# The transfer queue of a one-core attention and MLP kernel is put in the program's order

## The chip, the core and the metric

The kernel runs on one core of a Trainium2 chip. Its time is the device time of one launch in microseconds (us), the median of several runs. A core has five engines that each execute their own instructions in order: TensorE (PE in the profile; its weight loads are PEld), VectorE (DVE), ScalarE (ACT), GpSimd (POOL) and SyncE (SP). In this kernel SP computes nothing: it issues the transfers (DMAs), and SPq in the profile is its queue.

## What is computed

Attention with a top-32 mask over 8 batches, 8 heads, 576 rows and a head size of 64, and behind it a two-layer MLP with a smooth ReLU over 4608 tokens (512 to 2048 to 512), all in float32:

```python
scores = scale * np.matmul(q, k.transpose(0, 1, 3, 2))
kth = np.partition(scores, -top_k, axis=-1)[..., -top_k:-top_k + 1]
scores = np.where(scores >= kth, scores, -1000000000.0)
attn = np.exp(scores - np.max(scores, axis=-1, keepdims=True))
attn = attn / (np.sum(attn, axis=-1, keepdims=True) + 1e-09)
x = np.matmul(attn, v)                       # then (B, H, S, D) -> (B*S, H*D)
h = x @ w_in
g = np.where(h >= 1, h, np.where(h <= -1, 0.0, (h + 1) ** 2 / 4))
out = g @ w_out
```

## The kernel before

**Steps.** The work is cut into 144 steps. A step takes 128 query rows of one pair of heads. For each step PE computes the scores (`sp`, L354); ACT copies them to SBUF (`s`, L355) and takes the exponential (`e`, L391); DVE finds the 32 largest by repeated maxima and replacements (`more`, `less`, `tops`, L368 to L442) and masks the exponentials (L454); POOL divides by the sum (L407). Then the weights have to be transposed for the product with v (`po`, L502), whose result ACT copies into `xT` (L515). When a block of 128 tokens is complete, its MLP is queued: `ph` (L535), the activation by ACT (`r` L539, `g` L546) and POOL (L551 to L553), `py` (L558), and the output `y` (L561, L563).

**Early and late steps.** In the first steps PE transposes the weights, since it has time there while the MLP's own weights are being loaded and converted. In the late steps (about 144 to 1440 us) the transfers do it, in `move_w` (L480): ACT splits the weights into 16-bit halves (L484, two copies into the only buffer `halves`), a DMA writes them to DRAM (`rows`, L486), and a transposing DMA reads them back (`wT`, L488). Queries and keys of the batches from the third on go the same way in `turn` (L275): ACT's `parts` (L279), the write of `lines` (L281), and a transposing read into `qT` or `kT` (L282), which is kept in a list `turns` and issued by `finish_turns` (L286), either from `move_w` ahead of its own read or from slot 3 of a step.

**Inspection.** A late step of odd number also inspects a piece of the MLP's weights for values near zero: ACT reads the raw words twice (L172). The piece is loaded into a single buffer `raw` (L133); the call that loads it stands in slot 3 of the even step before (L770). There are 64 such pieces.

**Loads.** `load_values` (L189) is a generator: each `next` issues one group of the next batch's `v_in` or `v_tail`. `turned_keys_of` (L290) loads a `k_block` (three DMAs) and turns the one loaded before. `queries` (L680) turns a query block and calls `fetch` (L660), which loads the one after the next.

**The order.** The main loop (L737) goes through the steps, each in seven slots: slot 1 prepares queries and keys or values, slot 2 issues products with v and the scores of the step after the next, slot 3 has the inspection and `move_w` of the step before, and `advance` fills PE with MLP work in every slot. `tc.manual_schedule` (L654) makes PE, DVE, ACT and POOL execute their instructions in the order in which this loop writes them. SP is not on that list: a scheduler orders its transfers by their dependencies and its own estimates, and issues many loads well before the place at which the loop writes them.

Of the kernel before, what the change touches and what calls it, by code (L numbers as in the profile page):

```python
# [26 lines left out]
def kernel(  # L27
# [98 lines left out]
    def load(pool, i, bufs=3, parts=1):  # L126
        if i < n_pieces * parts and i not in loaded:
            if room:
                loaded[i] = room[i % len(room)]
            else:  # L130
                loaded[i] = pool.tile([P, 2 * WC // parts], U32, name="raw", bufs=min(bufs, 2))
            c = i % parts * (WC // parts)
            nc.sync.dma_start(out=loaded[i], in_=pieces_of_weights[i // parts][1][:, c:c + WC // parts].bitcast(U32))  # L133
# [42 lines left out]
    def run(ctx, paired):  # L176
# [104 lines left out]
            nc.sync.dma_start(out=lines, in_=parts)  # L281
            turns.append(partial(nc.sync.dma_start_transpose, dst.bitcast(U16), lines.rearrange("p t k -> (p t) k")))  # L282

        turns = []

        def finish_turns():  # L286
            while turns:
                turns.pop(0)()

        def turned_keys_of(b):  # L290

            kT = stage.tile([P, NHP, S], F32, name="kT")
            got = dict(kT=kT)

            def load_block(c):
                x = stage.tile([P, H, D], F32, name="k_block", tag="k_in")
                ends = k[b, :, SM:S, :].rearrange("h p d -> p h d")
                if c < NT:
                    nc.sync.dma_start(out=x[:, 0::2, :], in_=whole(k, b)[:, 0::2, c, :])
                    nc.sync.dma_start(out=x[TL:P, 1::2, :], in_=whole(k, b)[0:P - TL, 1::2, c, :])  # L300
                else:
                    nc.sync.dma_start(out=x[0:TL, 0::2, :], in_=ends[:, 0::2, :])
                nc.sync.dma_start(out=x[0:TL, 1::2, :], in_=whole(k, b)[P - TL:P, 1::2, c - 1, :] if c else ends[:, 1::2, :])
                return x

            blocks = {0: load_block(0)}
            got["loads"] = load_values(b)
            got["v"], got["v_tl"] = next(got["loads"])
            yield got
            for c in range(NT + 1):  # L310
                if c < NT:
                    blocks[c + 1] = load_block(c + 1)
                n = P if c < NT else TL
                turn(blocks.pop(c)[0:n], kT[:, :, c * P:c * P + n])
                yield got
# [164 lines left out]
        def move_w(st):  # L480
            st["wT"] = wT = late.tile([P, BLOCKS, P], F32, name="wT", bufs=4)
            halves = late.tile([P, 2, 2 * S], U16, name="halves")
            for i in range(2):
                nc.scalar.copy(halves[:, :, i * S:(i + 1) * S], st["e"][:, i, :].bitcast(U16).rearrange("p (k t) -> p t k", t=2))  # L484
            rows = dram.tile([P, 2, 2 * S], U16, name="rows")
            nc.sync.dma_start(out=rows, in_=halves)  # L486
            finish_turns()
            nc.sync.dma_start_transpose(wT.bitcast(U16), rows.rearrange("p t k -> (p t) k"))  # L488

        def block(i, c):  # L490
            return i * (NT + 1) + c if c < NT else NT
# [153 lines left out]
        def advance(amount, until):  # L645
# [4 lines left out]
            while pending and due >= pending[0][0] and pe_time < until and take():  # L650
# [1 line left out]
            due = min(due, 24.0)  # L652

        order = tc.manual_schedule(engines={mybir.EngineType.PE, mybir.EngineType.DVE, mybir.EngineType.Activation,  # L654
                                            mybir.EngineType.Pool})
        order.__enter__()
        keys, xTs = {}, {}
        q_ins, qTs = {}, {}
# [1 line left out]
        def fetch(i):  # L660
            if i < len(rounds) and rounds[i] not in q_ins:
                q_ins[rounds[i]] = load_queries(*rounds[i])
# [17 lines left out]
        def queries(m):  # L680
            nonlocal pe_time
            if m < n and steps[m][0:2] not in qTs:
                r = steps[m][0:2]
                if r[0] > 1:
                    qTs[r] = turned_queries_of(q_ins[r], r[1])
                else:
                    qTs[r] = queries_of(q_ins[r], r[1], nc.vector.tensor_copy if m == 0 else nc.scalar.copy)
                    pe_time += 0.5
                fetch(rounds.index(r) + 2)

        def begin(m):
            b, t, hp, ch, col = steps[m]
# [44 lines left out]
        for m in range(n + 2):  # L737
            early = converted < n_pieces
            if not early and first_late is None:
                first_late = m  # L740
            elif not early and late is None:
                conversion.close()
                room.clear()
                late = ctx.enter_context(tc.tile_pool(name="late", bufs=1))

            share, left = (total - spent) / (n + 2 - m), sum(x[0] for x in pending)
            for r in sorted(ready):
                if r + 4 > m and r >= valued:
                    share = min(share, left / (r + 4 - m))
                    left += NK * NF + NF * DM // P  # L750
            top_k, parts = None, [0] * SLOTS
            if m < n:
                top_k = weights(state[m], state[m - 1] if m > 0 else None, state[m + 1] if m + 1 < n else None)
                parts = [1] * SLOTS if early else [1, 1, 0, 1, 1, 1, 1]
                start = max(dve_time, scored[m])
                now_converting = range(0, SLOTS, 2)
                dve_time = start + K_TIME + PIECE_TIME * min(len(now_converting), n_pieces - converted)
                done[m] = dve_time
                state[m]["by_tensor"] = early or m >= n - 2
            for slot in range(SLOTS):  # L760
                now = start + (dve_time - start) * (slot + 1) / SLOTS
                for _ in range(parts[slot]):
                    next(top_k, None)
                if m < n and converted < n_pieces:
                    if slot in now_converting:
                        convert(now)
                elif slot == 3 and late is not None:
                    if m % 2:
                        inspect()
                    elif paired:  # L770
                        load(late, inspected, 1, 2)
                if slot == 1 and 1 <= m <= n and state[m - 1]["by_tensor"]:
                    pe_time = max(pe_time, done[m - 1] + 2.0) + 1.0
                    transpose_w(state[m - 1])
                    ready_at[m - 1] = pe_time + 1.8
                if slot == 3 and 1 <= m <= n and state[m - 1] is not None and not state[m - 1]["by_tensor"]:
                    move_w(state[m - 1])
                    ready_at[m - 1] = done[m - 1] + 15.0
                if slot == 3:
                    finish_turns()  # L780
                if slot == 2 and m == n and paired:
                    judge(ps, att)
                if slot == 2 and (early or m == first_late or m >= n - 1):
                    values_until(m)
                if m == 0 and slot in (1, 2):
                    next(first)
                if slot == 2 and not early:
                    if m % 2 == 0:
                        while pending and taken is not None and taken.__name__ == "hidden" and take():
                            pass  # L790
                    values_until((m - 2) // 2 * 2)
                if slot == (4 if early else 2):
                    begin_at(m + 2)
                if slot == (6 if early else 1):
                    queries(m + 3)
                    if (m < n and prep is None and next_keys < B and steps[m][0] == next_keys - 1 and steps[m][1] >= 1
                            and (next_keys > 1 or converted == n_pieces)):
                        prep = (turned_keys_of if next_keys > 1 else keys_of)(next_keys)
                    if prep is not None and (m % 2 == 0 or next_keys == 1):
                        got = next(prep, None)  # L800
                        pe_time += 0.5 if next_keys < 2 else 0.0
                        if got is None:
                            prep, next_keys = None, next_keys + 1
                        else:
                            keys[next_keys] = got
                            value_loads = got.get("loads", value_loads)
                    elif value_loads is not None:
                        next(value_loads, None)
                advance((EARLY_SHARE if early else share) / SLOTS if m < n else 32.0, now)
            for _ in (top_k if top_k is not None else ()):  # L810
                pass
# [50 lines left out]
```

## Time and profile before

| | us |
|---|---|
| median of 3 runs | 1506.48 (1506.18 to 1512.55) |
| the profiled execution, own time | 1507.81 |
| its span, first to last instruction | 1506.0 |
| PE, DVE, ACT, POOL busy | 1441.7, 1411.9, 1158.4, 908.5 |
| PEld busy (beside PE) | 1034.8 |
| SP's DMAs, share of 16 engines' span | 66.3% |

The profile is a page about one execution. Its first part gives the busy time of each engine, its fifth the groups of equal instructions (line, engine, operation, output and inputs, count; then busy time and mean ns of one; then the idle time just before them and what ended most of it), its sixth the DMA issues with the median time from issue to landing. Further views of the same trace are used below: busy time in stretches of the span; the waits of a stretch ("engine line waited for: us in total, times, longest"); and timelines of one engine, with the start and the duration of each instruction or row of equal ones. In SP's timeline a duration is that of the issue, not of the transfer: the data land later. A transposing read takes SP 2.3 to 3.4 us to issue, the write of `rows` 0.34 to 0.55.

The long middle of the run repeats every four steps in 38.3 us.

### The profile page before, as it was taken

What the parts mean: (1) busy time and instruction counts of PE and PEld (TensorE: products, weight loads), DVE (VectorE), ACT (ScalarE), POOL (GpSimd) and SP (SyncE); (2) the same over time, 40 slices, a digit from 0 to 9 for tenths busy, and PEclk for the clock granted to TensorE, in tenths of its full rate; (3) what the DMA queues carried; (4) which work ended last, traced back from release to release, by engine and by line L of the source; (5) the groups of instructions that cost most, each with busy time, mean ns of one, the idle gap of its engine ahead of it and who ended that gap; (6) DMA issues with size and microseconds to landing.
All of it is one profiled execution on the core that took longest, in us unless ns stands there. A gap on an engine that the chain in (4) does not pass through costs nothing.

```text
span 1506.0 us, 31908 instructions
## 1 busy us (share of the span) xinstructions
PE 1441.7 (96%) x10605; PEld 1034.8 (69%) x10605; DVE 1411.9 (94%) x4392; ACT 1158.4 (77%) x2221; POOL 908.5 (60%) x1309
## 2 busy tenths in 40 slices
PE   5698899999999999999999999999999999999998
PEld 3476577677777777677777777767777777777675
DVE  6989999999999999999999999999999999999912
ACT  6887788877778888687778888788778887877732
POOL 3463566666666666556666666666666666666630
PEclk6799899999999999999999999999999999999999
DMA  8632667785667787886677796787667877655510
GB/s 255 199 116 86 158 165 185 196 196 152 172 189 200 201 189 185 211 197 182 164 197 186 202 199 184 200 219 183 165 192 186 203 183 183 163 156 144 142 32 17
DMA packets 510318, 260.93 MB, mean 173 GB/s; under 512 B 460992, under 2 KB 469184, under 8 KB 510144
## 3 DMA queue, kind: packets, MB, share of 16 engines
q1 hardware_dynamic: 510144, 258.80, 66.3%
q8 instruction: 86, 1.41, 0.4%
q14 instruction: 88, 0.72, 0.1%
HBM read 62.91 MB, written 102.63 MB: 110 GB/s over the span
## 4 chain that ended last, share of the span: by engine, by line
PE 66%; DVE 20%; ACT 6%; DMA 3%; issue 3%; POOL 1%; SPq 1%; ACTq 0%; POOLq 0%
PE ph L535 24%; PE py L558 24%; PE sp L354 8%; PE po L502 8%; DVE more L375 5%; DVE e L454 4%; DVE less L368 2%; DVE more L368 2%; DMA rows<-halves 2%; PE pw L469 2%; DVE tops L416 2%; DVE tops L424 2%; DVE tops L435 2%; DVE seconds L442 2%; DVE tops L388 1%
## 5 line engine op out<-in xcount | busy, mean ns | idle before, releaser
L535 PEld LDWEIGHTS ph<-xT,w_in 128*128 128x128 f32 x4608 | 548.5, 193 | 100.0 <-issue 78.6
L535 PE MATMUL ph<-xT,w_in 128*128 128x128 f32 x4608 | 558.0, 277 | 1.3 <-ACT g L546 0.7
L558 PE MATMUL py<-w_out,g 128*128 128x512 f32 x1152 | 556.4, 603 | 1.7 <-ACT y L561 1.7
L551 POOL TENSOR_SCALAR r<-r 128x256 f32<-128x256 f32 x276 | 146.8, 532 | 453.6 <-ACT r L539 453.4
L375 DVE MATCH_REPLACE8 more<-tops,more 128x288 f32<-128x288 f32 x864 | 374.9, 437 | 0.0
L558 PEld LDWEIGHTS py<-w_out,g 128*128 128x128 f32 x1152 | 195.2, 190 | 166.9 <-issue 158.6
L484 ACT COPY halves<-e 128x1152 uint16<-128x1152 uint16 x268 | 293.6, 1143 | 13.4 <-DMA rows<-halves 13.4
L454 DVE SCALAR_TENSOR_TENSOR e<-s,kth,e 128x577 f32<-128x577 f32 x288 | 259.6, 937 | 0.8 <-ACT e L391 0.6
L553 POOL TENSOR_TENSOR g<-r,g 128x256 f32<-128x256 f32 x280 | 240.9, 860 | 22.0
L407 POOL TENSOR_SCALAR e<-e,rz 128x576 f32<-128x576 f32 x268 | 223.4, 843 | 12.6 <-DVE rz L400 12.6
L391 ACT ACTIVATE e<-s,nmax 128x576 f32<-128x576 f32 x288 | 222.5, 773 | 4.7
L539 ACT ACTIVATE r<-ph,half 128x256 f32<-128x256 f32 (+1 forms) x296 | 135.7, 458 | 116.4 <-PE ph L535 92.3
L355 ACT ACTIVATE s<-sp 128x576 f32<-128x576 f32 x288 | 171.9, 648 | 57.3 <-PE sp L354 55.6
L552 POOL TENSOR_TENSOR r<-r 128x256 f32<-128x256 f32 x276 | 190.1, 689 | 23.0
L354 PE MATMUL sp<-kT,qT 64*128 64x288 f32 x1024 | 164.1, 437 | 10.6 <-ACT kT L257 8.4
L502 PEld LDWEIGHTS po<-wT,v_in 128*64 128x64 f32 x2048 | 116.0, 139 | 60.5 <-ACT g L546 47.3
L502 PE MATMUL po<-wT,v_in 128*64 128x128 f32 x2048 | 142.1, 280 | 10.0 <-ACT g L546 6.5
L354 PEld LDWEIGHTS sp<-kT,qT 64*128 64x128 f32 x1024 | 89.7, 189 | 73.6 <-ACT r L539 28.0
L368 DVE TENSOR_TENSOR more<-s 128x576 f32<-128x576 f32 x144 | 112.3, 780 | 19.9 <-ACT s L355 19.9
L546 ACT ACTIVATE g<-ph,minus 128x256 f32<-128x256 f32 x280 | 129.8, 464 | 0.0
L416 DVE MAX8 tops<-more 128x8 f32<-128x288 f32 x288 | 125.4, 442 | 0.0
L368 DVE TENSOR_TENSOR less<-s 128x576 f32<-128x576 f32 x144 | 122.4, 850 | 0.0
(88 smaller groups left out, 1349.4 us busy)
## 6 DMA issues: line engine op xcount, KB each, us to landing
rows<-halves SPq DMA_DIRECT2D x134, 576.0 KB, 3.0
lines<-parts SPq DMA_DIRECT2D x48, 256.0 KB, 2.9
q_in<-in_q_dram SPq DMA_DIRECT2D x32, 256.0 KB, 3.7
v_in<-in_v_dram SPq DMA_DIRECT2D x32, 256.0 KB, 4.1
out_dram<-y SPq DMA_DIRECT2D x32, 256.0 KB, 2.8
raw<-in_moe_w_in_dram SPq DMA_DIRECT2D x32, 256.0 KB, 3.2
raw<-in_moe_w_out_dram SPq DMA_DIRECT2D x32, 256.0 KB, 3.3
kT<-in_moe_w_in_dram SPq DMA_DIRECT2D x8, 512.0 KB, 4.8
```

The source lines that it names most:

```text
L354: nc.tensor.matmul(*x, start=True, stop=True)
L368: nc.vector.tensor_tensor(out=x, in0=s[:, :, 0:SH], in1=s[:, :, SH:S], op=op)
L375: nc.vector.match_replace(out=st["rest"][:, i, :], in_to_replace=eight(st["tops"], i, r - 8), in_values=src[:, i, :], imm_value=LOWEST)
L391: nc.scalar.activation(e[:, i, :], s[:, i, :], AF.Exp, bias=nmax[:, i:i + 1])
L407: nc.gpsimd.tensor_scalar(st["e"][:, i, :], st["e"][:, i, :], rz[:, i:i + 1], 1.0, ALU.mult, ALU.mult)
L454: nc.vector.scalar_tensor_tensor(out=st["all"][1][:, i, :], in0=st["all"][0][:, i, :], scalar=last[i], in1=st["all"][1][:, i, :], op0=ALU. ...
L484: nc.scalar.copy(halves[:, :, i * S:(i + 1) * S], st["e"][:, i, :].bitcast(U16).rearrange("p (k t) -> p t k", t=2))
L502: nc.tensor.matmul(po[j * D:(j + 1) * D], v_in[:, h, c, :] if c < NT else v_tl[0][:, h, :], wT[:, block(j, c)], start=(c == 0), stop=(c == ...
L535: nc.tensor.matmul(ph[:, i], w_in[:, kk, f * P:(f + 1) * P], xT[:, kk], start=(kk == 0), stop=(kk == NK - 1))
L552: nc.gpsimd.tensor_tensor(out=r, in0=r, in1=r, op=ALU.mult)
L553: nc.gpsimd.tensor_tensor(out=g, in0=r, in1=g, op=ALU.add)
L558: nc.tensor.matmul(py[0], gs[f // group][:, f % group], w_out[:, f, :], start=(f == 0), stop=(f == NF - 1))
```

## The change

SP goes onto the list of engines whose order the loop lays out, and the loop places each kind of transfer by hand:

- the lists `turns`, `loads` and `reads` hold transfers that are written down at one place and issued at another, and `issue` empties one of them;
- the loads of keys, values and queries go into `loads`; slot 3 issues `turns` and then `loads`, behind `move_w` with its write of `rows`;
- the transposing read of `rows` goes into `reads`, which slot 5 issues;
- the load of the raw weight piece goes from slot 3 of the even step, ahead of `move_w`, to slot 5 of the same step, behind `reads`.

```diff
-        turns = []
-
-        def finish_turns():
-            while turns:
-                turns.pop(0)()
+        turns, loads, reads = [], [], []
+
+        def issue(x):
+            while x:
+                x.pop(0)()
...
-            blocks = {0: load_block(0)}
+            blocks = {}
+
+            def load_later(c):
+                loads.append(lambda: blocks.update({c: load_block(c)}))
+
+            load_later(0)
...
                 if c < NT:
-                    blocks[c + 1] = load_block(c + 1)
+                    load_later(c + 1)
...
             nc.sync.dma_start(out=rows, in_=halves)
-            finish_turns()
-            nc.sync.dma_start_transpose(wT.bitcast(U16), rows.rearrange("p t k -> (p t) k"))
+            reads.append(partial(nc.sync.dma_start_transpose, wT.bitcast(U16), rows.rearrange("p t k -> (p t) k")))
...
         order = tc.manual_schedule(engines={mybir.EngineType.PE, mybir.EngineType.DVE, mybir.EngineType.Activation,
-                                            mybir.EngineType.Pool})
+                                            mybir.EngineType.Pool, mybir.EngineType.SP})
...
-                fetch(rounds.index(r) + 2)
+                loads.append(partial(fetch, rounds.index(r) + 2))
...
                     if m % 2:
                         inspect()
-                    elif paired:
-                        load(late, inspected, 1, 2)
...
                 if slot == 3:
-                    finish_turns()
+                    issue(turns)
+                    issue(loads)
+                if slot == 5:
+                    issue(reads)
+                    if late is not None and paired and m % 2 == 0:
+                        load(late, inspected, 1, 2)
...
                     elif value_loads is not None:
-                        next(value_loads, None)
+                        loads.append(partial(next, value_loads, None))
```

The instructions of the four compute engines and their order stay as they are.

## The prediction

> **What bounds the kernel now.** I read the page first (busy shares and costliest groups), then busy time by stretches of 50 us, then the waits of single stretches, then the timelines of SP, ACT and PE between 706 and 748 us, which stand for the long middle of the run.
>
> ```profile
> PE 1441.7 (96%) x10605; PEld 1034.8 (69%) x10605; DVE 1411.9 (94%) x4392; ACT 1158.4 (77%) x2221; POOL 908.5 (60%) x1309
> L484 ACT COPY halves<-e 128x1152 uint16<-128x1152 uint16 x268 | 293.6, 1143 | 13.4 <-DMA rows<-halves 13.4
> ...
> rows<-halves SPq DMA_DIRECT2D x134, 576.0 KB, 3.0
> raw<-in_moe_w_in_dram SPq DMA_DIRECT2D x32, 256.0 KB, 3.2
> raw<-in_moe_w_out_dram SPq DMA_DIRECT2D x32, 256.0 KB, 3.3
> wT<-rows SPq DMA_TRANSPOSE x134, 5.0
> ```
>
> PE and DVE share the bound; ACT has 23% idle but every step's work passes through it in order. From 200 to 1440 us both PE and DVE are busy in nearly every microsecond, except in three stretches: PE has 48.14 of 50 us in 250–300, 46.35 in 600–650 and 46.92 in 950–1000, together 8.6 us short. The waits of 600–650 say why, and they also give the price of an ACT stall:
>
> ```profile
> PE po L502 <- ACT g L546: 3.2, 1, 3.2
> ACT halves L484 <- DMA rows<-halves: 3.1, 1, 3.1
> DVE more L368 <- ACT s L355: 2.7, 1, 2.7
> ```
>
> SP was issuing ten k and v loads in a row (617–626 us), so the write of `rows` left late, the single `halves` buffer came free late, and ACT stood still for 3.1 us between the weight inspection (L172) and the halves copy. PE then lost 3.2 us at its next `po`, DVE 2.7 us at its next `more`. So a stall of ACT at this place in a step goes through to PE almost one to one.
>
> **The change, part by part.** In the built kernels the instructions of PE, DVE, ACT and POOL keep their order; only SP's differs, with the same 746 DMAs. The sum is made against the profiled execution's own 1507.8 us (span 1506.0), 1.3 above the median 1506.5.
>
> *Loads spread out.* `v_in`, `v_tail` and `k_block` are now issued one group per step behind the `rows` write. The bursts, and the late `rows`, go: at most −8.6 us (the PE time missing in the three stretches), at least 0 if the new queue is as late there. I take −7, since PE also waits there for batch changes.
>
> *The transposing read of `rows`, two slots later.* It cannot start before `rows` has landed, 2.9 to 3.2 us after the write's issue (709.42 to 712.30, 738.52 to 741.68), so two slots of program order delay it by nothing in itself; `wT` lands 3.0 + 5.0 = 8 us after the halves are ready, 9.5 where a `kT` read and three `k_block` loads (1.25 + 1.66 us of issue) go ahead of it. The tightest reader, the second `po` at 730.15, comes 12 us after its `rows` (718.20). Cost 0, with 2.5 us of cover; beyond that it would hit PE one to one.
>
> *The `lines` write and the `qT` read of an odd step* now stand behind the even step's waiting `wT` read. The first `sp` that needs `qT` starts 4.4 us after the odd step's `rows` write (726.98 to 731.34); a `qT` read issued right behind it needs 0.35 + 3.3 = 3.7 us, up to 4.9 if `lines` lands late. So 0 to 0.5 us in the 18 of 30 query rounds that fall among key loads: 0 to 9, I take +3.
>
> *The raw weight load.* This is the large term. Before, SP issued it as soon as its one buffer was free; after, it is issued in the even step behind that step's `wT` read.
>
> ```profile
> 707.33 0.34 SPq L133 DMA_DIRECT2D raw<-in_moe_w_out_dram  x1
> ...
> 718.20 0.34 SPq L486 DMA_DIRECT2D rows<-halves  x1
> ...
> 721.45 3.40 SPq L488 DMA_TRANSPOSE wT<-rows  x1
> 724.94 1.25 SPq L288 DMA_TRANSPOSE qT<-lines  x1
> 726.29 0.53 SPq L133 DMA_DIRECT2D raw<-in_moe_w_out_dram  x1
> ...
> 738.52 0.35 SPq L486 DMA_DIRECT2D rows<-halves  x1
> 741.68 2.60 SPq L488 DMA_TRANSPOSE wT<-rows  x1
> ```
>
> ```profile
> 723.59 0.52 ACT L172 ACTIVATE raw<-raw,tiny 128x256 f32<-128x256 f32 x1
> ...
> 724.76 2.19 ACT L484 COPY halves<-e 128x1152 uint16<-128x1152 uint16 x2
> ...
> 727.89 0.46 ACT L546 ACTIVATE g<-ph,minus 128x256 f32<-128x256 f32 x1
> ...
> 744.31 0.52 ACT L172 ACTIVATE raw<-raw,tiny 128x256 f32<-128x256 f32 x1
> ```
>
> ```profile
> 725.48 3.60 PE L558 MATMUL py<-w_out,g 128*128 128x512 f32 x8
> 729.01 1.09 PE L502 MATMUL po<-wT,v_in 128*64 128x128 f32 x16
> ```
>
> The piece read at 723.59 was requested at 707.33, 16 us ahead. In the new order the request follows `rows` (718.20), its landing (+3.0) and the issue of the `wT` read (+2.5, during which SP takes nothing else): 5.6 us after `rows`. It lands some 2.7 us later (between 2.5 and the median 3.3), 8.3 us after `rows`. ACT wants it 5.4 us after `rows` here and 5.8 us after it in the next pair (738.52 to 744.31). ACT so stalls 2.9 and 2.5 us, in front of the halves copy, the second exponential and the `r`, `g` pair on which PE's `po` waits. PE has 0.66 us of cover at the first place (`g` ends at 728.35, `po` at 729.01) and none at the second (in the same stretch PE's `po` waits for `g` up to 0.9 us already): it loses 2.2 and 2.5, 2.3 on average. DVE has no more cover than in 600–650 and follows. Behind SP's waiting read there are besides the raw load only the output store and `lines`.
>
> There are 64 such loads, one for every second step, 144 to 1361 us; the first has no `wT` read ahead of it. Between 335 and 916 us, 31 have the distances above: 31 × 2.3 = 71. After 930 us ACT comes later (raw reads at 1093.31 and 1111.74 against `rows` at 1086.2 and 1105.5: 7.1 and 6.2 us), so it stalls 1.2 and 2.1 and PE, with 0.1 and 0.7 of cover, loses 1.2: 23 × 1.2 = 28. The nine before 320 us meet PE with idle time left (44.89 of 50 in 150–200): between 0 and 2.7 each, I take 0.9: 8. In 28 pairs a `kT` read or `k_block` loads stand between `rows` and `wT`; they outlast the landing by 0.35 and slow the transposing read, as `q_in` does at 721.45 (3.40 against 2.5): 0 to 1.4, I take 0.7: 20. In sum 71 + 28 + 8 + 20 + 3 − 7 = +123.
>
> [...]
>
> Bounds of the raw term: low, if half of it is made up by ACT's later waits for PE (2.0 us at `xT`, 1.3 at `r`): 31 × 1.2 + 23 × 0.5 = 49; high, with no cover and all surcharges: 31 × 2.9 + 23 × 2.1 + 9 × 2.7 + 28 × 1.4 = 202. With −8.6 to 0 and 0 to 9 for the rest: +40 to +211.
>
> **Rivals.** *Hidden (faster).* ACT is idle for 23% and catches up before PE or DVE needs it; only the three stalls go: 1506.5 − 8.6 = 1498. For it: ACT's idle share, and DVE seldom waits for ACT. Against it: ACT's waits for PE come after the stalled place and depend on PE, which would itself be late; the 3.1 us stall at 625.9 was not hidden.
>
> *Half hidden.* PE and ACT settle into a new rhythm in which ACT's waits shrink: 64 × 0.8 − 7 = +44, 1550. For it: from one `rows` to the next ACT needs some 9 us against 9.56 of the average step. Against: PE has no idle time left with which to catch up.
>
> *Only turn reads are late.* The raw load lands in time after all and `qT` costs 30 × 0.3 = 9 against −7: 1508, decided by whether `lines` lands before the odd step's `rows` write.
>
> That the change does not do what it says is excluded for the order, which is that of the built program.
>
> **How the numbers follow.** Raw wait in full 0.70, 1507.8 + 123 − 1.3 = 1630 (its own range 1547 to 1700); half hidden 0.12; hidden 0.14; turn reads 0.04. About 0.5%, or 7.5 us, can be told from no change: faster needs under 1499, slower over 1514. Faster 0.10 (most of the hidden case, whose 1498 lies near the border), same 0.07 (its rest and most of the turn reads), slower 0.83. The range 1530 to 1690 leaves out the faster cases, the extreme high end and part of the half-hidden case.
>
> **What would show it.** Right: a wait "ACT raw L172 <- DMA raw" of 1 to 3 us some 60 times, 100 to 160 us in total; "PE po <- ACT g" growing from 6.5 + 47.3 by about as much; PE's share near 89%; raw issues 0.1 us behind a `wT` read; and no 13.4 us at L484. Wrong: ACT waits at L172 without PE waiting (hidden), raw landing within 5.5 us of `rows`, or new waits of `sp` for `qT` or of `po` for `wT` larger than those for `g`.

## The result and the profile after

| | before | after |
|---|---|---|
| median, us | 1509.51 (4 runs) | 1768.84 (1764.31 to 1778.15, 4 runs) |
| profiled span, us | 1506.0 | 1764.7 |
| PE busy, us | 1441.7 | 1523.0 |
| PE idle in the span, us | 64.3 | 241.7 |
| DVE busy, us | 1411.9 | 1422.7 |

The changed kernel is slower: its time is 1.171 of that before (95% interval 1.169 to 1.174). The prediction had +123 us and a range up to 1690; measured are some +259. Of the 258.7 us by which the span grew, 177.4 are idle time of PE and 81.3 are additional busy time of PE, with the same 10605 matmuls. Lines of the changed kernel's page follow: the busy shares, the granted clock of PE in 40 slices of the span (PEclk, in tenths of full speed), and four of the costliest groups.

```profile
PE 1523.0 (86%) x10605; PEld 1101.5 (62%) x10605; DVE 1422.7 (81%) x4392; ACT 1161.9 (66%) x2221; POOL 867.6 (49%) x1309
...
PEclk6898999999999889898998998999999999999999
...
L489 ACT COPY halves<-e 128x1152 uint16<-128x1152 uint16 x268 | 294.8, 1142 | 2.1 <-POOL e L412 0.5
L359 PE MATMUL sp<-kT,qT 64*128 64x288 f32 x1024 | 183.2, 478 | 97.8 <-DMA qT<-lines 91.2
...
L506 PE MATMUL po<-wT,v_in 128*64 128x128 f32 x2048 | 159.0, 302 | 59.4 <-ACT g L550 57.3
L172 ACT ACTIVATE raw<-raw,tiny 128x256 f32<-128x256 f32 x128 | 68.3, 533 | 209.0 <-DMA raw<-in_moe_w_in_dram 110.0
```

Two of the same groups before:

```profile
L354 PE MATMUL sp<-kT,qT 64*128 64x288 f32 x1024 | 164.1, 437 | 10.6 <-ACT kT L257 8.4
L502 PE MATMUL po<-wT,v_in 128*64 128x128 f32 x2048 | 142.1, 280 | 10.0 <-ACT g L546 6.5
```

ACT's 13.4 us of waits for `rows` at the halves copy are gone but for 0.5, as the prediction expected of the spread loads. In their place ACT waits 209 us ahead of the inspection (L172). PE waits for `qT` and for `g`, and one `sp` matmul now takes 478 ns on average, against 437 before. The waits of the changed kernel over the whole span:

```profile
DVE more L373 <- ACT s L360: 140.3, 68, 3.8
...
DVE e L459 <- ACT e L396: 126.6, 72, 5.1
...
ACT raw L172 <- DMA raw<-in_moe_w_in_dram: 110.0, 30, 7.3
ACT raw L172 <- DMA raw<-in_moe_w_out_dram: 96.9, 30, 6.8
PE sp L359 <- DMA qT<-lines: 91.2, 23, 6.3
...
PE po L506 <- ACT g L550: 57.3, 22, 5.1
```

60 of the 64 inspections wait, 206.9 us in all, 3.45 on average. One such pair of steps in the timelines of SP, ACT and PE:

```profile
791.73 0.36 SPq L491 DMA_DIRECT2D rows<-halves  x1
792.18 1.47 SPq L288 DMA_TRANSPOSE kT<-lines  x1
794.95 2.56 SPq L288 DMA_TRANSPOSE wT<-rows  x1
797.56 0.57 SPq L133 DMA_DIRECT2D raw<-in_moe_w_out_dram  x1
798.23 0.38 SPq L281 DMA_DIRECT2D lines<-parts  x1
804.49 0.33 SPq L491 DMA_DIRECT2D rows<-halves  x1
804.91 1.60 SPq L288 DMA_TRANSPOSE qT<-lines  x1
```

```profile
801.10 0.53 ACT L172 ACTIVATE raw<-raw,tiny 128x256 f32<-128x256 f32 x1 [3.83 <-DMA raw<-in_moe_w_out_dram]
...
802.27 2.19 ACT L489 COPY halves<-e 128x1152 uint16<-128x1152 uint16 x2
```

```profile
804.60 0.39 PE L506 MATMUL po<-wT,v_tail 128*64 128x128 f32 x4
808.86 2.29 PE L359 MATMUL sp<-kT,qT 64*128 64x288 f32 x8 [3.88 <-DMA qT<-lines]
811.08 3.78 PE L539 MATMUL ph<-xT,w_in 128*128 128x128 f32 x16
814.65 2.80 PE L562 MATMUL py<-w_out,g 128*128 128x512 f32 x6
817.29 1.95 PE L539 MATMUL ph<-xT,w_in 128*128 128x128 f32 x16
```

`rows` leaves at 791.73, the `wT` read 3.2 us later, and the raw request only when that is issued, at 797.56, 5.8 us behind `rows`. ACT gets the piece at 801.10 and has stood still for 3.83 us. Its halves copy is late by that, so the next `rows` leaves at 804.49, and behind it on SP stands the `qT` read, whose `lines` had been sent off at 798.23. PE, which this time did not wait at `po`, waits 3.88 us for `qT`. Then comes what the prediction did not have at all: eight `sp` matmuls take 2.29 us instead of 1.24, sixteen `ph` 3.78 instead of 1.95. The granted clock of the same stretch (columns: window; length; busy time with counts for PE, PEld, DVE, ACT, POOL; granted PE clock; DMA share; GB/s):

```profile
804.00:808.00 4.00, 0.99 (x19) 0.74 (x14) 3.79 (x14) 2.18 (x6) 2.25 (x4) 0.99 0.71 206
808.00:810.00 2.00, 1.14 (x6) 0.94 (x8) 1.22 (x6) 0.00 (x0) 1.37 (x3) 0.50 0.81 181
810.00:812.00 2.00, 2.00 (x10) 1.24 (x7) 0.13 (x1) 1.30 (x2) 0.00 (x0) 0.50 1.72 159
812.00:814.00 2.00, 2.00 (x11) 2.00 (x11) 2.00 (x5) 0.00 (x0) 0.00 (x0) 0.50 0.45 89
814.00:816.00 2.00, 2.00 (x8) 1.29 (x7) 2.00 (x10) 1.01 (x4) 0.40 (x1) 0.81 0.24 53
816.00:820.00 4.00, 4.00 (x22) 2.55 (x20) 2.23 (x5) 4.00 (x6) 3.53 (x6) 1.00 0.10 39
```

After the wait PE runs on half its clock until about 814.8 us, and loses 2.9 us more. The trace records every change of the granted clock, so this loss can be summed: over the whole span PE was busy for 208.6 us on half the clock, against 44.1 before. Half of the difference is 82 us, which is all of the 81.3 by which its busy time grew.

### The profile page after: what moved, and what is told of

It reads as the page before. It is cut to its first block, busy times and chain, and to the rows that moved or that the text cites. A ratio compares the mean times of both kernels' runs of the same rounds, so it can differ in the third digit from the quotient of the medians.

```text
span 1764.7 us, 31827 instructions
## 1 busy us (share of the span) xinstructions
PE 1523.0 (86%) x10605; PEld 1101.5 (62%) x10605; DVE 1422.7 (81%) x4392; ACT 1161.9 (66%) x2221; POOL 867.6 (49%) x1309
## 3 DMA queue, kind: packets, MB, share of 16 engines
q8 instruction: 86, 1.41, 0.3%
## 4 chain that ended last, share of the span: by engine, by line
PE 54%; DMA 19%; ACT 16%; SPq 6%; issue 4%; POOL 0%; DVE 0%; ACTq 0%; POOLq 0%
PE ph L539 19%; PE py L562 18%; PE sp L359 9%; ACT halves L489 7%; PE po L506 6%; DMA raw<-in_moe_w_in_dram 5%; DMA qT<-lines 5%; DMA raw<-in_moe_w_out_dram 5%; SPq L288 4%; ACT raw L172 3%; DMA rows<-halves 2%; PE pw L474 1%; ACT e L396 1%; ACT s L360 1%; ACT r L543 1%
## 5 line engine op out<-in xcount | busy, mean ns | idle before, releaser
L539 PEld LDWEIGHTS ph<-xT,w_in 128*128 128x128 f32 x4608 | 578.6, 201 | 116.1 <-issue 71.2
L539 PE MATMUL ph<-xT,w_in 128*128 128x128 f32 x4608 | 589.3, 286 | 10.0 <-ACT xT L521 4.1
L555 POOL TENSOR_SCALAR r<-r 128x256 f32<-128x256 f32 x276 | 133.3, 483 | 754.2 <-ACT r L543 754.2
L359 PE MATMUL sp<-kT,qT 64*128 64x288 f32 x1024 | 183.2, 478 | 97.8 <-DMA qT<-lines 91.2
L412 POOL TENSOR_SCALAR e<-e,rz 128x576 f32<-128x576 f32 x268 | 242.3, 913 | 10.0 <-DVE rz L405 10.0
L506 PE MATMUL po<-wT,v_in 128*64 128x128 f32 x2048 | 159.0, 302 | 59.4 <-ACT g L550 57.3
L172 ACT ACTIVATE raw<-raw,tiny 128x256 f32<-128x256 f32 x128 | 68.3, 533 | 209.0 <-DMA raw<-in_moe_w_in_dram 110.0
L359 PEld LDWEIGHTS sp<-kT,qT 64*128 64x128 f32 x1024 | 100.9, 207 | 163.6 <-issue 106.4
L506 PEld LDWEIGHTS po<-wT,v_in 128*64 128x64 f32 x2048 | 131.4, 153 | 111.1 <-ACT g L550 80.3
L556 POOL TENSOR_TENSOR r<-r 128x256 f32<-128x256 f32 x276 | 180.3, 653 | 23.0
```

Of the source, the lines that this page charges most:

```text
L359: nc.tensor.matmul(*x, start=True, stop=True)
L412: nc.gpsimd.tensor_scalar(st["e"][:, i, :], st["e"][:, i, :], rz[:, i:i + 1], 1.0, ALU.mult, ALU.mult)
L506: nc.tensor.matmul(po[j * D:(j + 1) * D], v_in[:, h, c, :] if c < NT else v_tl[0][:, h, :], wT[:, block(j, c)], start=(c == 0), stop=(c == ...
L539: nc.tensor.matmul(ph[:, i], w_in[:, kk, f * P:(f + 1) * P], xT[:, kk], start=(kk == 0), stop=(kk == NK - 1))
L556: nc.gpsimd.tensor_tensor(out=r, in0=r, in1=r, op=ALU.mult)
```

## The experiments

Ratios are to the kernel before, run on the same chip in the same set; idle is the span less the busy time of PE.

| kernel | ratio (95%) | median, us | PE busy | PE idle | ACT waits for raw, or work added | PE waits for `qT` |
|---|---|---|---|---|---|---|
| changed | 1.171 (1.169–1.174) | 1768.8 | 1523.0 | 241.7 | 206.9 | 91.2 |
| e1 | 0.9973 (0.9959–0.9986) | 1509.6 | 1443.7 | 65.0 | 0.4 | 5.6 |
| e2 | 1.031 (1.027–1.036) | 1560.7 | 1454.2 | 105.4 | none | 37.7 |
| e3 | 1.129 (1.123–1.134) | 1706.5 | 1487.9 | 210.8 | 262.1 | 6.9 |
| e4 | 1.030 (1.028–1.032) | 1558.2 | 1457.1 | 100.9 | 3.3 | 24.0 |
| e5 | 1.0036 (1.0022–1.005) | 1515.3 | 1440.3 | 72.5 | none | 8.6 |
| e6 | 1.218 (1.214–1.221) | 1838.5 | 1560.9 | 274.9 | 251 added | 87.7 |
| e7 | 1.046 (1.043–1.049) | 1578.9 | 1448.2 | 128.6 | 84 added | 32.5 |
| e8 | 0.9984 (0.997–0.9998) | 1507.1 | 1445.8 | 63.0 | 0.2 | 6.4 |
| e9 | 1.177 (1.174–1.180) | 1780.0 | 1570.8 | 209.6 | 216.9 | 54.5 |
| e10 | 1.037 (1.033–1.041) | 1567.1 | 1459.8 | 106.4 | 58.0 | 29.2 |
| e11 | 1.010 (1.008–1.012) | 1526.8 | 1445.1 | 78.3 | 0.8 | 19.3 |
| e12 | 1.120 (1.117–1.124) | 1691.5 | 1489.1 | 200.5 | 169 added | 59.7 |

**e1: the raw request back to its old place.**

```diff
                     if m % 2:
                         inspect()
+                    elif paired:
+                        load(late, inspected, 1, 2)
...
                     issue(reads)
-                    if late is not None and paired and m % 2 == 0:
-                        load(late, inspected, 1, 2)
```

> The changed kernel with one part undone: the raw weight piece is again requested in slot 3 of the even step, ahead of the write of rows, instead of in slot 5 behind the transposing read. Theory (the late raw piece is the one cause, PE's waits for qT and its lower clock follow from it): ACT's waits for raw fall from 207 us to under 10, PE's waits for qT from 91 to under 15, the granted clock is 0.99 or more from 200 us on, and the time is 1495 to 1515. Rival (the order of SP's queue as a whole: reads that wait hold up lines and the qT read): the waits for raw go, those for qT stay at 70 to 100, and the time stays over 1600.

Measured: 1509.6 us, 0.4 us of waits for raw, 5.6 us for `qT`, a clock of 1.00 between 200 and 1440 us. One transfer's place is worth 259 us. The rest of the change together makes the kernel some 0.3% faster than before (by the interval, 0.1 to 0.4%). Busy time of e1 in the three stretches in which PE lost time before (columns as above):

```profile
250.00:300.00 50.00, 49.61 (x380) 35.37 (x377) 50.00 (x155) 41.05 (x79) 33.29 (x50) 1.00 0.93 216
600.00:650.00 50.00, 47.59 (x356) 34.07 (x355) 47.34 (x150) 38.94 (x76) 30.80 (x47) 0.97 0.78 205
950.00:1000.00 50.00, 49.97 (x380) 35.43 (x379) 50.00 (x156) 42.50 (x81) 34.94 (x51) 1.00 0.95 232
```

PE has 5.8 us more there than before (49.61, 47.59, 49.97 against 48.14, 46.35, 46.92). Over the whole span its idle time is 65.0 us against 64.3 before, so in these two profiles the gain is given back elsewhere.

**e2: the same queue, the raw piece read a step later. e5: e2's reading with e1's queue.**

```diff
-                    if m % 2:
-                        inspect()
+                    if m % 2 == 0 and inspected in loaded:
+                        inspect()
```

> SP's order is that of the changed kernel, transfer for transfer; only ACT's inspection of a raw piece moves from the odd step to slot 3 of the next even step, so that the piece has a step more to arrive. Theory (late raw piece): no waits for raw, few for qT, 1495 to 1520. Rival (order of the queue): the queue is the same, so waits for qT of 70 to 100 us and over 1600.

> The compute engines' order is that of e2 (inspection in even steps); the raw request stands where e1 has it, ahead of the write of rows, instead of behind the transposing read. It tells what of e2's 50 us comes from the queue and what from ACT's order. If the raw request between the wT read and the lines write is the cost (queue): 1505 to 1525, waits of ACT parts for lines under 5 us and of PE for qT under 15. If inspecting in even steps is the cost (it shortens the time between an even and an odd write of rows by 1.2 us): 1545 to 1565, with qT waits of 30 or more as in e2 (37.7).

In e5 the inspection of e2 is followed in slot 3 by the raw load, and slot 5 has none. Measured: e2 1.031, e5 1.0036. So e2 showed that no single wait for raw is left and still 3% are lost; e5 takes nearly all of it back by moving the request alone. The waits of e2:

```profile
PE sp L359 <- DMA qT<-lines: 37.7, 21, 3.8
ACT parts L279 <- DMA lines<-parts: 29.8, 13, 3.5
```

Issued between the `wT` read and the `lines` write, the raw request also makes `lines` late, and through it `qT`: from 340 us on `lines` is issued 4.8 us after ACT has finished `parts` in e2, against 4.1 in e5 (means), and takes 3.25 us to land against 2.62 (medians). In e5 the waits for `qT` are 8.6 us and those of ACT for `lines` 14.0; the second was expected under 5. The expected time of e2 was too low. Its rival, the queue, was right in kind, but with 37.7 us of waits for `qT` instead of 70 to 100, and with a fifth of the whole loss. The later inspection by itself costs 0.6% (e5 against e1).

**e3: the turns ahead of `rows`.** In slot 3 `issue(turns)` is also called ahead of `move_w`.

> The changed kernel, with the transposing reads of qT and kT issued ahead of the write of rows in slot 3 instead of behind it; the raw piece stays late. Theory (qT waits because the late raw piece makes the rows write late, behind which the ready qT read stands): waits for raw stay at 180 to 220, waits for qT fall below 40, a part of the gain is lost again to waits of PE for g and of DVE for ACT, 1650 to 1740. Rival (qT waits are a second cost of their own, independent of raw): all of 91 us and the clock lost behind them come back, 1600 or less.

```profile
ACT raw L172 <- DMA raw<-in_moe_w_in_dram: 135.0, 31, 9.2
ACT raw L172 <- DMA raw<-in_moe_w_out_dram: 127.1, 32, 8.0
...
PE po L506 <- ACT g L550: 102.2, 23, 7.3
...
PE sp L359 <- DMA qT<-lines: 6.9, 3, 3.1
```

84 us of waits for `qT` are gone, and 62 us of the time; the waits for raw have grown by 55, past the 220 that were expected at most, and those of PE for `g` by 45. Of the 66 us by which the span is shorter, 31 are idle time of PE and 35 its work on half the clock. PE's waits for `qT` are a second face of ACT's stall (the `qT` read stands behind the late `rows`), in part with a price of its own.

**e4: SP in program order, nothing placed by hand.** The kernel before with `mybir.EngineType.SP` added to the list.

> The kernel before with one edit: SP put on the list of engines in program order, nothing placed by hand. The raw request then stands in slot 3 of the even step ahead of rows; the transposing read of wT right behind its rows. Theory (only the raw piece's place costs): no raw waits, 1495 to 1530. Rival (a waiting SP in program order costs by itself): over 1550.

Measured 1558 us, as the rival had it (over 1550): 3.3 us of waits for raw, but PE waits 24.0 us for `qT`, DVE 52.9 for `s`, and the stretch 600 to 650 us has only 42.92 us of PE. Program order costs 3% here unless the transfers are placed in it; all of the change's other placing (e1) takes that back and 0.3% more. Which placing takes back how much was not taken apart, except for the `wT` read (e11).

**e10: the raw request still in slot 5, but ahead of the `wT` read.** The two statements of slot 5 change places.

> The changed kernel with two statements of slot 5 exchanged: the raw request is issued ahead of the transposing read of wT instead of behind it, still behind the write of rows and the loads. Theory (only SP's standing still at that read makes raw late): raw is issued 0.4 to 2.4 us after rows and lands 3.7 to 5.8 us after it, against the 5.4 to 7.2 at which ACT wants it: waits for raw under 20 us (now 207), 1508 to 1525. Rival (anywhere behind rows is too late): waits of 60 us or more and 1560 or more.

Measured 1.037, with 58.0 us of waits for raw. The greater part of the loss is SP's standing still at the transposing read, but behind `rows` and the loads is too late too, in 27 places. Where `k_block` loads go ahead of it, it is issued at 826.83 for a `rows` of 824.17, say, and read at 832.44, after a wait of 3.23 us. The time is 42 us above the range of the theory; the rival had it, and nearly its waits (60 or more).

**e11: e1 with the `wT` read in slot 3, ahead of the loads.**

> e1 with the transposing read of wT issued in slot 3, behind the turns and ahead of the loads, instead of in slot 5. It tells what the two slots are worth once raw is in time. Since the read waits for rows to land in either place, and only the loads change sides: within 0.4% of e1 (0.9973 of the kernel before), that is 0.994 to 1.002. Rival (loads behind the waiting read land too late for ACT's parts or for k): over 1.01, with waits of ACT parts for k_block or q_in.

Measured 1.010, outside what was expected. The loads now stand behind the waiting read and push the next `lines` back: it is issued 4.5 us after `parts` is finished instead of 4.0 (means from 340 us on). PE waits 19.3 us for `qT` instead of 5.6. The rival had the time, but ACT waits for `k_block` only 1.5 us. So the two slots that the transposing read was moved are worth 1.3%, by what may go ahead of it.

**e6, e7, e12: the stall made by ACT's own work.** e1's transfers, with the two passes of the inspection repeated:

```diff
-        for x in range(2):
+        for x in list(range(2)) * 4:
```

(2 in e7, 3 in e12.) The repeated passes write the same values.

> e1 (raw piece in time), with the inspection's two passes executed four times instead of once: 3 x 1.17 = 3.5 us more of ACT work at the place where the changed kernel waits 3.45 us on average for raw. SP's order is that of e1. Theory (a stall of ACT at this place is enough for the whole loss): 1700 to 1780, qT waits of PE 60 or more, granted clock 0.93 to 0.96 between 200 and 1440 us. Rival (part of the loss needs the late raw load in SP's queue): under 1660, clock 0.98 or more.

> As e6, with the two passes executed twice: 1.17 us more of ACT work in each odd step. If the loss is proportional to the stall: a third of e6's, some 75 to 90 us, 1580 to 1600. If short stalls are partly covered and leave the clock alone, and long ones lower it: 64 x (1.17 - 0.35 of cover) = 52 at the most, 1525 to 1560, and a granted clock of 0.99 or more between 200 and 1440 us.

> As e6 and e7, with the inspection's two passes executed three times: 2.34 us more of ACT work in each of 64 odd steps, 150 us in all. In e7 (75 us) the loss was 0.92 of the work at an unchanged clock, in e6 (225 us) 1.46 of it with PE's clock at 0.90 between 200 and 1440 us. If PE's clock falls only behind waits of some 3 us and more, as the trace of the changed kernel has it: PE's gaps are 2 to 2.7 us here, few of them lower the clock, and the price stays at 0.9 to 1.1 of the work: 1645 to 1675, clock 0.97 or more. If the price rises evenly with the stall: 1.2 of it, 1690, clock 0.95.

The expectations count 1.17 us for each repetition; measured it is 1.31, since an inspection takes ACT 1.17 us in e1, 2.49 in e7, 3.82 in e12 and 5.10 in e6 (medians, from the first pass to the halves copy). In 64 steps that makes 84, 169 and 251 us more in e7, e12 and e6. Against e1, PE's idle time grows by 64, 136 and 210 us: 0.76, 0.80 and 0.84 of the added work. PE's busy time grows by 4.5, 45 and 117 us; half of the growth of its work on half the clock is 3, 45 and 120. So the idle part is nearly proportional to the stall, and a second part comes in with its length. The stall alone, with raw in time, makes a loss of the size of the changed kernel's, `qT` waits included. In e6 it is larger, past the 1780 that were expected at most, as its stall (3.9 us each time) is longer than that of the changed kernel (3.45). e7 came out at 1579 us, between its two cases (1580 to 1600 for a proportional loss, 1525 to 1560 for short stalls that are partly covered), with a clock of 1.00 between 200 and 1440 us, as in the second. Two lines of PE from e7 and then two from e6, behind a short and a long wait:

```profile
467.80 1.24 PE L359 MATMUL sp<-kT,qT 64*128 64x288 f32 x8 [1.47 <-DMA qT<-lines]
468.97 2.05 PE L539 MATMUL ph<-xT,w_in 128*128 128x128 f32 x16
```

```profile
507.15 1.70 PE L359 MATMUL sp<-kT,qT 64*128 64x288 f32 x8 [4.07 <-DMA qT<-lines]
508.78 3.20 PE L539 MATMUL ph<-xT,w_in 128*128 128x128 f32 x16
```

Counted over PE's timelines of the changed kernel, e6, e7 and e12 from 200 to 1640 us (a wait counts as followed by slow work when the `sp`, `po` and `ph` of the next 9 us are together over 0.5 us longer than usual):

| PE waits | followed by slow work | in the changed kernel |
|---|---|---|
| 0.9 to 2 us | 1 of 59 | 0 of 6 |
| 2 to 3 us | 32 of 73 | 8 of 15 |
| over 3 us | 79 of 85 | 33 of 33 |

By this count the slow work makes 72 us in the changed kernel, of the 81 by which PE's busy time grew. e12's time is that of its rival, an even rise, its clock (0.97) that of its theory: most of its waits are 2.5 to 2.7 us long and lie in the band where 32 of 73 were followed by slow work, which the theory had expected of waits of some 3 us and more.

**e9: filling a part of the waits for `qT`.** 16 transposes of the identity on PE ahead of the first `sp` of each late query round.

> The changed kernel with 16 transposes of the identity matrix put on PE ahead of the first scores of each of the 30 late query rounds, into the same PSUM tile, which the scores overwrite: 2 us of PE work in place of 2 of the some 4 us in which PE waits for qT there. Every transfer and wait stays. Theory (after a wait of 3 us and more PE runs on a lower granted clock for some us, which is where the 81 us of additional PE busy time come from): the shortened waits leave the clock up, qT waits fall from 91 to 30 to 50, PE's share of the loss shrinks and the time falls by 25 to 60 us in spite of 60 us more PE work, to 1705 to 1745. Rival (the clock follows something else, such as the load of the chip, and the waits alone set the time): unchanged within 10 us, or slower.

```profile
805.68 1.97 PE L349 MATMUL sp<-ident 128*128 128x128 f32 x16
810.38 1.24 PE L361 MATMUL sp<-kT,qT 64*128 64x288 f32 x8 [2.74 <-DMA qT<-lines]
811.55 2.05 PE L541 MATMUL ph<-xT,w_in 128*128 128x128 f32 x16
```

Here, where the changed kernel has 2.29 and 3.78, `sp` and `ph` run at full speed behind the shortened wait. But 11 of the 26 waits for `qT` of a late round that are left were still 2.4 to 3.2 us long, and 10 of them were followed by slow work. PE's busy time without the filler (30 × 1.97) is 1511.7, only 11 us less, ACT's waits for raw grew by 10 and the time was 1.177. The filler did not do what was expected: the time is that of the rival, though not for the rival's reason (a clock that follows something else), since it is still the work behind the waits that is slow. The expected effect is seen in single places only.

**e8: the value loads behind the `wT` read, on top of e1.**

> e1 with the value loads issued behind the transposing read of wT instead of ahead of it, since in e1 one of them waits for PE's last product of the batch before (595.41 us) and holds up wT, lines and qT behind it; 600 to 650 us has 47.34 us of DVE there. Theory: that stretch gains 2 us, 1 to 4 us under e1, ratio to the kernel before 0.994 to 0.997. Rival (DVE and PE bind there by themselves): as e1, 0.997.

The stretch of 600 to 650 us gained (PE 48.87, DVE 49.63 us), the time did not: 0.9984 against 0.9973 of e1, with intervals that overlap. e1 and e8 are the versions that beat both kernels, the one before by 0.2 to 0.3%; they can't be told apart.

## Why the prediction was wrong

**What held.** The direction and the cause: the raw request behind SP's waiting read. Its arithmetic of places held for the plain pairs: issued 5.6 us behind `rows` by the prediction, 5.4 and 5.8 at 824.17 and 797.56. ACT's stall goes through to PE nearly whole: the prediction had some 0.9 (0 to 0.7 us of cover on 2 to 2.9), the changed kernel shows 177 of 207, 0.86. The spread loads brought PE 5.8 us in the three stretches of e1, for which 7 was taken; that the whole run gains as much is not shown. PE's `po` waits for `wT` only 0.8 us.

**The size of the stall.** The step "It lands some 2.7 us later (between 2.5 and the median 3.3)" took the low end; the median after is 3.2 and 3.3, and at 797.56 it took 3.5. The surcharge for pairs with a `kT` read or `k_block` loads was taken as 0.7 us; after the first ten pieces the request leaves 6.7 us behind `rows` in 31 such pairs and 5.4 in the 23 others, 1.2 later. And the nine pieces that the prediction has before 320 us, priced at 8 us together, stall ACT by 40. The stall is 3.45 us on average instead of 1.2 to 2.9. Summed over the prediction's rows ACT's stalls come to about 150 us (31 × 2.7, 23 × 1.65 and the smaller terms), against 207: of the gap of 136 us to the measured +259 in the span this explains some 50.

**The term that was missing.** "In sum 71 + 28 + 8 + 20 + 3 − 7 = +123" has only idle time. PE's busy time was taken as fixed. This is the step that failed: it grew by 81 us, since behind 41 of the 48 waits of over 2 us PE's work was slow, and PE was busy for 208.6 us on half its clock. The prediction's range lay below the result for this reason: the high end of the raw term, 202, plus 81 is more than the measured 259. The trace of before had the sign in the view that the prediction quotes: 600 to 650 us, the stretch with the 3.1 us stall, has a granted clock of 0.97 where the next has 1.00.

```profile
600.00:650.00 50.00, 46.35 (x346) 33.18 (x346) 46.64 (x145) 38.22 (x73) 28.83 (x43) 0.97 0.87 212
650.00:700.00 50.00, 49.97 (x360) 35.22 (x359) 50.00 (x154) 38.99 (x74) 31.52 (x45) 1.00 0.77 189
```

**The face of the loss.** "So 0 to 0.5 us in the 18 of 30 query rounds" priced the `qT` read against an odd step's `rows` that leaves on time. That `rows` is the first thing that ACT's stall delays; with it PE's waits for `qT` were 91 us. The prediction looked for PE's loss at `po`, where it grew from 6.5 to 57.3 only. Waits for `qT` larger than those for `g` were among its own signs of being wrong, and that sign came. In e6, where raw is in time, the loss takes the same two forms (87.7 and 83.5).

**The slots of the transposing read,** "Cost 0": right for the changed kernel against the one before, whose scheduler had put loads ahead of such reads too (`q_in` at 720.92); but against SP in program order the two slots are worth 1.3% (e11).

**Smaller slips.** The bounds add up to 1547 to 1717, not 1700. Between 617 and 626 us SP issued eight loads and a `kT` read; the other two of the ten loads stand at 611 and 613, ahead of a `wT` read. The raw piece of the `rows` at 1105.5 is read at 1111.64, not 1111.74. And the issue times given ahead of the prediction hold for `wT` and `rows` in the stretches shown only: over the whole run before, the read of `wT` takes SP 2.2 to 5.2 us (median 2.5), those of `qT` and `kT` 1.2 to 2.5, the write of `rows` 0.33 to 1.41. None of these moves the +123 us.

## What to carry over

When one queue is put into program order, go through what stands behind each of its waiting transfers and ask when that is wanted: here a load with one buffer and 16 us of lead lost all of it to a read that waits for a landing. A stall on a helper engine that passes through to a saturated TensorE cost here 0.76 to 0.86 of its own length in idle time, and in the changed kernel a further 72 us of slow work, behind 41 of its 48 gaps of over 2 us and none of its 6 of 0.9 to 2; so the length of the single gap mattered here, not their sum alone. And a transfer that is "ready" was late where its issue stood behind one that was not: the `qT` read at 804.91, behind the `rows` of 804.49, with its `lines` sent off at 798.23.

## What the runs showed of the hardware

PE's granted clock is either full or half (1.00 or 0.50) in the traces of the kernels before and after. In the changed kernel it is half 40 times between 200 and 1640 us, 25 times for 3.41 us and 15 times for 6.83. Sixteen `ph` took 3.78 us on it, against 1.95 on the full clock. It was half while PE was still waiting, too: from 807.95 us on, 0.9 us ahead of the late `sp`.

Waits of nearly the same length differ in what follows them. Two of e12, of 2.58 and 2.63 us:

```profile
398.73 1.24 PE L359 MATMUL sp<-kT,qT 64*128 64x288 f32 x8 [2.58 <-DMA qT<-lines]
399.90 3.68 PE L539 MATMUL ph<-xT,w_in 128*128 128x128 f32 x16
...
442.67 1.24 PE L359 MATMUL sp<-kT,qT 64*128 64x288 f32 x8 [2.63 <-DMA qT<-lines]
443.84 2.05 PE L539 MATMUL ph<-xT,w_in 128*128 128x128 f32 x16
```

The granted clock of the stretch around the first (columns as above):

```profile
396.00:398.00 2.00, 0.15 (x4) 0.00 (x0) 2.00 (x11) 0.27 (x1) 1.84 (x4) 1.00 1.04 252
398.00:400.00 2.00, 1.27 (x9) 0.88 (x9) 1.23 (x6) 0.48 (x1) 1.38 (x3) 1.00 0.79 179
400.00:402.00 2.00, 2.00 (x10) 2.00 (x11) 1.25 (x2) 1.97 (x5) 0.00 (x0) 0.51 1.08 195
402.00:404.00 2.00, 2.00 (x10) 1.76 (x9) 2.00 (x7) 2.00 (x4) 0.00 (x0) 0.63 0.76 186
```

Behind the first wait the clock is 0.51 between 400 and 402 us, and the sixteen `ph` take 3.68 us, though PE had been busy for 1.42 us of the 4 us before; behind the second they take 2.05. No run was made to tell what makes the difference between two such waits.
